# Two feed-forward networks behind a clustered attention: the order of instructions written out as a list

## The chip, the cores and the metric

One core of a Trainium2 chip. The metric is the device time of one execution in microseconds (us), as the median of several runs; lower is better. Engines: TensorE (PE), VectorE (DVE), ScalarE (ACT), GpSimd (POOL) and SyncE (SP), which issues the loads.

## The reference

```python
x = attention(q, k, v)              # 2 x 8 heads, 768 tokens, masked by clusters
h = x @ w_in                        # x: 1536 x 512, w_in: 512 x 2048
g = where(h >= 1, h, where(h <= -1, 0, (h + 1)**2 / 4))
x = g @ w_out                       # 1536 x 512
xn = x / sqrt(mean(x*x) + 1e-6) * rms_g
g = silu(xn @ w_gate) * (xn @ w_val)    # 512 x 1536 each
out = g @ w_out2                    # 1536 x 512
```

Everything is float32.

## The kernel before, in words

The attention takes up to about 250 us and isn't touched. Behind it stand two feed-forward networks (FFN), layers 1 and 2. Each factor is split into a high part that the multiplier takes (type fp32r) and a low rest, and a product is three matmuls: high by high, high by low, low by high. The tokens are three blocks of 512 (b = 0, 1, 2), the hidden columns slices of 128 (m).

*Units.* TensorE's work is a list of units. `h_unit` computes one slice for one block (12 matmuls of 512 columns). For blocks 0 and 1 `term_unit` computes a Strassen-like scheme: seven products of six matmuls each (called k = 1, 5, 2, 6, 3, 7, 4), added up in three PSUM banks A, B and E. Partial sums are copied out by ScalarE as u (after k = 1), e (5), v (6) and w (7, line 918), and added by DVE or POOL later (lines 924, 929). Product 3 adds to the bank E and so needs the copy e first; product 6 needs u, 7 needs v, 4 needs w. In layer 2, `half_unit` does the same for the halves of block 2 with 256 columns (names with h; copies in line 963). `y_unit` multiplies a group of slices with the second weight for 128 tokens (lines 1128 to 1130; y1 and y2; groups of 3, 4, 3, 3, 3 slices, and of 2), and the result is added to Y by DVE (line 1144; the first by a copy of ScalarE, line 1142). Between the layers come the norm (lines 1169 to 1174, 1181) and transposes of Y (xt, line 1066).

*Helpers.* Each unit leaves tasks for the other engines: gate or silu, the rounding to the high part by ScalarE (line 866) and the low rest by DVE (line 864), copies and additions. Weights come in as raw and mid by SyncE's loads (line 549), and are converted by two activations of ScalarE (lines 722, 723) and five steps of DVE (lines 724 to 728; into places named aa, bb or place); the last step of a conversion issues the load two places on (`load_next`). Sums of weights for the scheme are made by POOL (lines 739, 754, 755) and rounded (lines 716, 717).

*What sets the order.* `ORDER` permutes the units. The helpers are ordered by a planner: `KINDS` gives each operation an engine, a duration and a lag, each task has a due time, and before each unit `run` issues all operations that by its clock could have started, the one with the earliest due time first. A unit whose factor isn't planned yet pulls it in with `wait_for`, and `refill` begins the next weight conversion as soon as there is a place.

```python
    while unit():
        pass
    run(1e9)
```

PSUM has six banks of tag h (A, E, h, y, xt) and two of tag B; the buffers of other kinds are few (two of raw and mid each, four of u). An engine waits for a buffer's last reader in the order in which it was issued.

Of the kernel before, what the change touches and what calls it, by code (L numbers as in the profile page):

```python
# [32 lines left out]
SHARED, XP = 0.8, 1  # L33
KEEP, YD, GD, ROUND, XD, END4 = 1.5, 6.0, 6.0, 6.0, 2.0, 0.0
ORDER = (
# [21 lines left out]
NEAR, DUE, CONV = 0.1, 8.0, 4.0  # L57
LOAD, LAND = 4.2, 0.8
# [8 lines left out]
def clustered_attention_two_ffn(  # L67
# [509 lines left out]
    def conv(n_ops=1):  # L577

        for _ in range(n_ops):
# [12 lines left out]
            while cv["loaded"] < cv["limit"] and cv["loaded"] <= cv["at"]:  # L592
# [10 lines left out]
    def due_of(key):
        at = pace["pe"]
        for u in work:
            if key in u[3]:
                return at - CONV
            at += u[1]
        return at

    def task(ready, *ops, late=0.0, end=None, due=None):

        due = ready + DUE if due is None else due
        tasks.append(SimpleNamespace(ready=ready, ops=list(ops), late=late, end=end, due=due))

    def op(kind, f, sets=(), needs=(), stage=0):
        return kind, f, sets, needs, stage

    spans = {"dve": [], "pool": []}

    def start_of(x):
        kind, _, _, needs, _ = x.ops[0]
        e = KINDS[kind][0]
        at = max([clock[e], x.ready, *(known[k] for k in needs)])
        other = "pool" if kind in ("ttl", "t2l", "tiny") else "dve" if e == "pool" else None
        for a, b in spans[other][-3:] if other else ():
            if a <= at < b:
                at += SHARED * (b - at)
        return at

    def emit(x):
        kind, f, sets, needs, stage_ = x.ops[0]
        for k in needs:
            want(k)
        e, busy, lag = KINDS[kind]
        at = start_of(x)
        x.ops.pop(0)
        f()
        clock[e] = at + busy
        if e == "pool" or kind in ("ttl", "t2l", "tiny"):  # L640
            spans[e].append((at, at + busy))
        x.ready = at + lag
        if x.ops and x.ops[0][4] > stage_:
            x.due += ROUND
        for k in sets:
            known[k] = x.ready
        if not x.ops:
            tasks.remove(x)
            if x.end:
                x.end()  # L650

    def want(key):
        while key not in known:
            x = [x for x in tasks if any(key in o[2] for o in x.ops)]
            assert x, key
            emit(x[0])
        return known[key]

    def wait_for(*keys):
        for k in keys:  # L660
            pace["pe"] = max(pace["pe"], want(k) + 0.1)

    def run(until):
        while True:
            refill()
            heads = {}
            for n, x in enumerate(tasks):
                if any(k not in known for k in x.ops[0][3]):
                    continue
                at = start_of(x)  # L670
                if at < until:
                    heads.setdefault(KINDS[x.ops[0][0]][0], []).append((at, n, x))
            best = None
            for e, xs in heads.items():
                first = min(a for a, _, _ in xs) + NEAR
                a, n, x = min((y for y in xs if y[0] <= first), key=lambda y: (y[2].due, y[1]))
                if best is None or a < best[0]:
                    best = a, x
            if best is None:
                break  # L680
            emit(best[1])
# [12 lines left out]
    def load_next():
        while cv["loaded"] < len(stream) and stream[cv["loaded"]][2] < 0:
            cv["loaded"] += 1
        n = cv["loaded"]
        if n < len(stream):
            layer, i, m = stream[n]
            b = bound.setdefault("bits", [])  # L700
            bind("bits", 3, None)
            w_load()
            clock["dma"] = max(clock["dma"], pace["pe"] + 1.0) + LOAD
            landed[n] = clock["dma"] + LAND

    landed = {}

    def make():
# [13 lines left out]
        task(landed[n], op("copy", lambda: nc.scalar.activation(sq, hi.bitcast(F32), AF.Copy, scale=2.0 ** -112), (("y", n),)),  # L722
# [870 lines left out]
    for k in known:  # L1593
        known[k] = 0.0
# [70 lines left out]
```

## Time and profile before

| | us |
|---|---|
| median of 3 runs | 780.74 (780.57 to 780.75) |
| profiled execution | 779.35 |
| its span in the profile | 777.4 |
| PE busy in it | 763.2 (98%) |
| DVE busy | 630.2 (81%) |
| ACT busy | 468.0 (60%) |
| POOL busy | 330.3 (42%) |
| PE's granted clock, mean | 0.998 |

The span reaches from the first instruction to the last; 1.95 us of the profiled execution lie around it. PE is busy nearly all the time, so a seam is found by the starts of its matmuls: where they follow one another at the steady distance, PE loses nothing.

### The profile page before, as it was taken

Reading aid. Unit: us, or ns where it says so; the run is one execution under the profiler, and the core shown is the slowest. Engines: PE = TensorE matmul, PEld = TensorE weight load, DVE = VectorE, ACT = ScalarE, POOL = GpSimd, SP = SyncE. Lnnn points to the kernel's source line nnn. Section 1 sums busy time; section 2 is a strip of 40 time slices with the busy share of each in tenths; the row PEclk is TensorE's granted clock in tenths of the full one; section 3 lists DMA queues with packets and bytes.
Section 4 is the critical chain, followed back from the end, with each engine's and each line's share of the span. In section 5 each row is a group of like instructions: output and inputs, shape, how many; then the busy total and the mean of one; then the engine's idle time right before and its main releaser. Section 6 shows DMA issues by size and latency. Waiting matters only on the chain.

```text
span 777.4 us, 11522 instructions
## 1 busy us (share of the span) xinstructions
PE 763.2 (98%) x3897; PEld 593.0 (76%) x3897; DVE 630.2 (81%) x1164; ACT 468.0 (60%) x930; POOL 330.3 (42%) x344
## 2 busy tenths in 40 slices
PE   8999999999999989999999999899999999999998
PEld 4666676766558767888888888688888888888886
DVE  6776787776677979888889999999998798888545
ACT  6676767665565769548548358667754536365250
POOL 5878999998000050330400036455524333341220
PEclk9999999999999999999999999999999999999999
DMA  7757665572143155443452620336535344442004
GB/s 193 180 139 183 154 159 127 144 183 100 55 162 122 31 187 177 149 162 109 162 174 99 225 100 2 109 109 207 172 136 188 111 152 124 140 154 82 0 1 163
DMA packets 32682, 103.45 MB, mean 133 GB/s; under 512 B 5016, under 2 KB 5356, under 8 KB 32624
## 3 DMA queue, kind: packets, MB, share of 16 engines
q1 hardware_dynamic: 32612, 102.72, 43.5%
q8 instruction: 31, 0.51, 0.3%
q14 instruction: 27, 0.22, 0.1%
q10 hardware_dynamic: 12, 0.00, 0.0%
HBM read 81.02 MB, written 3.15 MB: 108 GB/s over the span
## 4 chain that ended last, share of the span: by engine, by line
PE 74%; DVE 16%; ACT 6%; issue 2%; DMA 1%; POOL 0%; DVEq 0%; ACTq 0%; POOLq 0%
PE B L848 9%; PE pv L432 8%; PE y L1130 7%; PE y L1128 7%; PE y L1129 7%; PE mp L362 5%; PE E L848 4%; PE sc L411 4%; PE sc L412 4%; PE h L789 3%; PE A L848 2%; DVE a L839 2%; PE sum L451 1%; DVE Y L1144 1%; ACT a L828 1%
## 5 line engine op out<-in xcount | busy, mean ns | idle before, releaser
L364 DVE TENSOR_REDUCE M<-mp 128x1 f32<-128x384 f32 x186 | 94.5, 552 | 44.5 <-PE mp L362 44.3
L424 POOL TENSOR_TENSOR acc<-acc,P 128x384 f32<-128x384 f32 x112 | 109.5, 1016 | 4.1 <-ACT P L414 3.5
L414 ACT ACTIVATE P<-sc 128x384 f32<-128x384 f32 x192 | 82.4, 490 | 41.7 <-PE sc L412 36.2
L739 POOL TENSOR_TENSOR bits<-aa 128x512 f32<-128x512 f32 x16 | 23.0, 1440 | 159.7 <-DVE aa L728 152.9
L1144 DVE TENSOR_TENSOR Y<-y,Y 128x512 f32<-128x512 f32 (+1 forms) x109 | 73.0, 678 | 8.9 <-PE y L1130 8.4
L432 PE MATMUL pv<-P,v 128*64 128x384 f32 x384 | 70.6, 492 | 0.0
L929 POOL TENSOR_TENSOR w<-w,e 128x512 f32<-128x512 f32 x17 | 24.2, 1422 | 108.3 <-ACT w L918 108.3
L411 PE MATMUL sc<-aa,bb 112*128 112x384 f32 x192 | 66.2, 345 | 0.0
L412 PE MATMUL sc<-aa,bb 97*128 97x384 f32 x192 | 65.0, 338 | 0.0
L789 PE MATMUL h<-xh,aa 128*128 128x512 f32 x200 | 64.3, 391 | 0.1
L739 POOL TENSOR_TENSOR bits<-place 128x512 f32<-128x512 f32 x13 | 18.3, 1407 | 85.5 <-DVE place L728 79.8
L362 PE MATMUL mp<-bb,aa 112*128 112x384 f32 x186 | 52.5, 360 | 0.2
L722 ACT ACTIVATE raw<-raw 128x512 f32<-128x512 f32 x62 | 41.5, 677 | 13.3 <-DMA raw<-w_out 6.9
L432 PEld LDWEIGHTS pv<-P,v 128*64 128x64 f32 x384 | 25.4, 136 | 31.5 <-issue 30.5
L789 PEld LDWEIGHTS h<-xh,aa 128*128 128x128 f32 x200 | 37.5, 188 | 9.9 <-DVE a L839 0.8
L362 PEld LDWEIGHTS mp<-bb,aa 112*128 112x128 f32 x186 | 32.2, 189 | 15.2 <-issue 5.5
L723 ACT ACTIVATE raw<-raw 128x512 f32<-128x512 f32 x62 | 41.8, 679 | 1.1
L789 PE MATMUL h<-xl,aa 128*128 128x512 f32 x100 | 39.0, 390 | 0.0
L411 PEld LDWEIGHTS sc<-aa,bb 112*128 112x128 f32 x192 | 36.3, 189 | 3.3 <-ACT P L414 1.4
L412 PEld LDWEIGHTS sc<-aa,bb 97*128 97x128 f32 x192 | 36.3, 189 | 0.0
L724 DVE TENSOR_SCALAR mid<-mid 128x512 uint32<-128x512 uint32 x62 | 33.5, 547 | 2.5 <-DMA mid<-w_out 1.8
L725 DVE TENSOR_SCALAR bits<-raw 128x512 uint32<-128x512 uint32 x62 | 34.3, 557 | 1.4 <-ACT raw L722 1.4
(678 smaller groups left out, 2239.2 us busy)
## 6 DMA issues: line engine op xcount, KB each, us to landing
raw<-w_out SPq DMA_DIRECT2D x28, 512.0 KB
mid<-w_out SPq DMA_DIRECT2D x28, 511.8 KB
raw<-w_in SPq DMA_DIRECT2D x16, 512.0 KB
mid<-w_in SPq DMA_DIRECT2D x16, 511.8 KB
raw<-w_gate SPq DMA_DIRECT2D x12, 512.0 KB
raw<-w_val SPq DMA_DIRECT2D x12, 512.0 KB
mid<-w_gate SPq DMA_DIRECT2D x12, 511.8 KB
mid<-w_val SPq DMA_DIRECT2D x12, 511.8 KB
```

The costliest lines, as they stand in the source:

```text
L362: nc.tensor.matmul(mp, A[0:112, h, 0, 128 * qt:128 * qt + 128], Bk[0:112, h, 0, HALF * n:HALF * n + HALF], start=True, stop=True)
L364: nc.vector.tensor_reduce(st["M2", p][:, j, n:n + 1], mp, axis=AX.X, op=ALU.max)
L411: nc.tensor.matmul(sc, Bk[0:112, h, 0, ks], A[0:112, h, 0, qs], start=True, stop=False)
L412: nc.tensor.matmul(sc, Bk[0:97, h, 1, ks], A[0:97, h, 1, qs], start=False, stop=True)
L414: nc.scalar.activation(P, sc, AF.Exp, scale=0.125)
L424: nc.gpsimd.tensor_tensor(acc, acc, P, op=ALU.add)
L432: nc.tensor.matmul(pv[64 * h:64 * h + 64, 0:HALF], st["v", p][:, h, kt], st["P", p, i, h], start=(kt == 0), stop=(kt == NT - 1))
L789: nc.tensor.matmul(h, w[:, wi, fs], x[:, kc, cs], start=(n == 0), stop=(n == 11))
L848: nc.tensor.matmul(h[:, 0:x[xi].shape[2]], w[:, wi, fs], x[xi][:, kc], start=start and n == 0, stop=(n == 5), skip_group_check=not start)
L1128: nc.tensor.matmul(y[:, c], g[:, 0, fs], w[:, 0, c], start=(m == m0), stop=False)
L1129: nc.tensor.matmul(y[:, c], g[:, 0, fs], w[:, 1, c], start=False, stop=False)
L1144: nc.vector.tensor_tensor(Y[:, c], y[:, c], Y[:, c], op=ALU.add)
```

## The change

The planner goes. A tuple `ISSUE` of some 2,000 numbers says what is issued next: `U` the next unit, `M` the next weight conversion (its tasks are made), and a number n the next operation of task n (tasks count from 0 in the order in which they are made). `ORDER`, the order of the units, is another one in places. The distances by which a needed value must be known are now asked for exactly: `have` replaces `wait_for`, and a layer 2 product needs only the part of x that it reads (`x_key`).

```diff
-SHARED, XP = 0.8, 1
-KEEP, YD, GD, ROUND, XD, END4 = 1.5, 6.0, 6.0, 6.0, 2.0, 0.0
+UNIT, MAKE = -1, -2
+U, M = UNIT, MAKE
+ISSUE = (
+    M, M, U, U, U, U, U, U, 25, 11, 25, 15, 10, 8, U, 25, 10, 11, 27, 11, 7, 26, 11, U, 8, 28, 13, 26, 19, 25,
...
+    620, U, 621, U, 622, U, 623, U, 624, U, 625)
 ORDER = (
...
-    253, 254, 255, 256, 258, 257, 259, 260, 261, 262, 263, 264, 270, 265, 266, 267, 268, 269, 272, 273, 271,
...
+    255, 256, 270, 258, 257, 259, 260, 261, 262, 263, 264, 265, 266, 267, 268, 269, 272, 273, 271, 274, 276,
...
-    def task(ready, *ops, late=0.0, end=None, due=None):
...
+    def task(*ops, end=None):
+
+        tasks[made[0]] = SimpleNamespace(ops=list(ops), end=end)
+        made[0] += 1
...
+    def emit(n):
+        x = tasks[n]
+        f, sets, needs, _ = x.ops.pop(0)
+        have(*needs)
         f()
...
+        known.update(sets)
         if not x.ops:
-            tasks.remove(x)
+            del tasks[n]
             if x.end:
                 x.end()
...
+    def have(*keys):
+        assert not pace["on"] or known.issuperset(keys), keys
...
+    def x_key(k, t):
+        return {1: ("tp0", t), 2: ("tp0", t), 3: ("xd", t)}.get(k) or ("xl", t, {5: 0, 6: 1, 7: 2, 4: 3}[k])
...
-            wait_for(*((("xl" if k in (5, 6, 7, 4) else "xd"), t) for t in range(4)))
+            have(*(x_key(k, t) for t in range(4)))
...
-    while unit():
-        pass
-    run(1e9)
-    assert not tasks
+    for n in ISSUE:
+        if n == UNIT:
+            work.pop(0)[0]()
+        elif n == MAKE:
+            make()
+        else:
+            emit(n)
+    assert not work and not tasks
```

Only the order of instructions differs. Line numbers above 700 are some 3 to 25 lower after the change (848 is 827, 1066 is 1044, 1128 is 1103; 722 is 725). Three places show it.

ScalarE at the slice pair m = 3 of layer 1 (the names end in a running number; e1_3 is the copy e, v1_3 the copy v, a1_3_2 the gated slice 3 of block 2, bb0 the place of its high part). Before:

```order
L723 ACTIVATE raw11_3331<-raw11_3331 128x512
L828 ACTIVATE a1_3_2_3441<-h1_3_2_3414,half_b_93 128x512
L835 ACTIVATE a1_3_2_3441<-a1_3_2_3441 128x512
L866 CAST bb0_106<-a1_3_2_3441 128x512
L918 COPY e1_3_3458<-E1_3_3451 128x512
L828 ACTIVATE a1_3_0_3473<-A1_3_3433,half_b_93 128x512
L722 ACTIVATE raw12_3408<-raw12_3408 128x512
L918 COPY v1_3_3470<-B1_3_3397 128x512
```

ScalarE at the same place after the change:

```order
L726 ACTIVATE raw15_3388<-raw15_3388 128x512
L898 COPY e1_3_3461<-E1_3_3454 128x512
L1014 CAST place1_3129<-p3_0_3291 128x512
L807 ACTIVATE a1_3_2_3474<-h1_3_2_3425,half_b_93 128x512
L898 COPY v1_3_3473<-B1_3_3409 128x512
L814 ACTIVATE a1_3_2_3474<-a1_3_2_3474 128x512
L807 ACTIVATE a1_3_0_3487<-A1_3_3442,half_b_93 128x512
L814 ACTIVATE a1_3_0_3487<-a1_3_0_3487 128x512
L898 COPY w1_3_3503<-B1_3_3409 128x512
L1014 CAST place1_3129<-p3_1_3313 128x512
L719 CAST aa0_105<-s1_5_1_3440 128x512
L807 ACTIVATE a1_3_1_3512<-E1_3_3454,half_b_93 128x512
```

The copy e1_3 stood behind the gate and the rounding of a1_3_2 (L866, CAST). Now the gate stands behind the copy, and the rounding follows two rows below the last one shown. Between come a weight's two activations and casts of x parts (L1014).

TensorE at the norm (layer 2; B_0 and B_1 belong to slices 0 and 1, the two xt are the transposes of Y's tiles 8 and 10, of 128 tokens each). Before:

```order
L848 MATMUL B_0_5305<-aa_109,place_3131 128x512
L1066 MATMUL xt_5393<-ident_f,Y 128x128 x4
L1066 MATMUL xt_5398<-ident_f,Y 128x128 x4
L848 MATMUL B_1_5414<-xh,place_3133 128x512
L848 MATMUL B_1_5414<-xl,place_3133 128x512
L848 MATMUL B_1_5414<-xh,place_3133 128x512 x2
L848 MATMUL B_1_5414<-xl,place_3133 128x512
```

TensorE there after the change:

```order
L827 MATMUL B_1_5393<-xh,place_3133 128x512
L827 MATMUL B_1_5393<-xl,place_3133 128x512
L827 MATMUL B_1_5393<-xh,place_3133 128x512 x2
L827 MATMUL B_1_5393<-xl,place_3133 128x512
L827 MATMUL B_1_5393<-xh,place_3133 128x512
L827 MATMUL A_1_5406<-xh,place_3133 128x512
L827 MATMUL A_1_5406<-xl,place_3133 128x512
L827 MATMUL A_1_5406<-xh,place_3133 128x512 x2
L827 MATMUL A_1_5406<-xl,place_3133 128x512
L827 MATMUL A_1_5406<-xh,place_3133 128x512
L1044 MATMUL xt_5415<-ident_f,Y 128x128 x4
L1044 MATMUL xt_5420<-ident_f,Y 128x128 x4
```

The transposes stood directly behind the last unit of slice 0 and now stand behind the first two units of slice 1 (B_1 and A_1), each of six matmuls.

TensorE at the half products of slices 0 and 1. Before:

```order
L848 MATMUL B_0h<-bb_106,place_3131 128x256 x6
L848 MATMUL B_0h<-bb_108,place_3129 128x256 x6
L848 MATMUL B_1h<-xh,place_3133 128x256
L848 MATMUL B_1h<-xl,place_3133 128x256
L848 MATMUL B_1h<-xh,place_3133 128x256 x2
L848 MATMUL B_1h<-xl,place_3133 128x256
L848 MATMUL B_1h<-xh,place_3133 128x256
L848 MATMUL A_1h<-xh,place_3133 128x256
```

TensorE there after the change:

```order
L827 MATMUL B_0h<-bb_106,place_3131 128x256 x6
L827 MATMUL B_1h<-xh,place_3133 128x256
L827 MATMUL B_1h<-xl,place_3133 128x256
L827 MATMUL B_1h<-xh,place_3133 128x256 x2
L827 MATMUL B_1h<-xl,place_3133 128x256
L827 MATMUL B_1h<-xh,place_3133 128x256
L827 MATMUL B_0h<-bb_108,place_3129 128x256 x6
L827 MATMUL A_1h<-xh,place_3133 128x256
```

The third and fourth product in the bank B_0h followed each other directly; now B_1h's first product stands between them. In the same way y2_0_4, the first unit of y2, now stands between B_1h's last two products. Other moves on TensorE: E2_0 stands ahead of A2_0; the first unit of each later pair (B2_4, B2_6, B2_8, B2_10) stands ahead of the y2 group that it used to follow for seven units; the second unit of B2_11 stands ahead of E2_11h. Up to the norm TensorE's order is the same, and so is that of SyncE's loads throughout.

## Rows read from the trace of the kernel before

**Rows 1.** The page, busy time of each engine (share of the span), instructions:
```profile
PE 763.2 (98%) x3897; PEld 593.0 (76%) x3897; DVE 630.2 (81%) x1164; ACT 468.0 (60%) x930; POOL 330.3 (42%) x344
```

**Rows 2.** PE's waits, 238 to 778 us: total, times, longest:
```profile
PE xt L1066 <- DVE Y L1181: 2.9, 1, 2.9
PE E L848 <- ACT e L918: 2.9, 1, 2.9
PE B_0h L848 <- ACT w_0h L963: 1.0, 1, 1.0
PE B_1h L848 <- ACT w_1h L963: 0.5, 1, 0.5
...
```

**Rows 3.** PE in stretches: width, busy (instructions), granted clock, DMA share, GB/s:
```profile
290.00:300.00 10.00, 10.00 (x45) 1.00 0.31 106
255.88:265.31 9.43, 9.02 (x38) 1.00 0.01 2
282.31:289.80 7.49, 4.64 (x19) 1.00 0.69 216
307.49:311.29 3.80, 3.28 (x14) 1.00 0.65 225
436.45:438.97 2.52, 2.33 (x10) 1.00 0.28 86
493.59:496.72 3.13, 3.02 (x13) 1.00 0.82 285
496.72:508.39 11.67, 8.74 (x41) 0.85 0.01 4
501.00:504.00 3.00, 2.83 (x11) 0.50 0.02 5
507.60:508.39 0.79, 0.79 (x9) 1.00 0.00 0
519.10:521.85 2.75, 1.70 (x14) 1.00 0.60 191
521.85:525.51 3.66, 3.66 (x32) 1.00 0.13 19
525.51:527.72 2.21, 1.69 (x14) 1.00 0.69 248
574.26:574.99 0.73, 0.73 (x3) 1.00 0.24 90
```

**Rows 4.** ScalarE's timeline at E1_3 and at B_1h: start, duration, line, operation:
```profile
281.95 0.63 ACT L835 ACTIVATE a<-a 128x512 f32<-128x512 f32 x1
285.52 0.62 ACT L866 CAST bb<-a 128x512 fp32r<-128x512 f32 x1 [2.94 <-DVE a L839]
286.05 0.58 ACT L918 COPY e<-E 128x512 f32<-128x512 f32 x1
...
526.48 0.37 ACT L963 COPY w_1h<-B_1h 128x256 f32<-128x256 f32 x1 [0.31 <-PE B_1h L848]
```

**Rows 5.** PE's timeline, 500 to 503 us:
```profile
501.17 1.94 PE L1066 MATMUL xt<-ident_f,Y 128*128 128x128 f32 x8 [2.93 <-DVE Y L1181]
```

**Rows 6.** VectorE's timeline at the end of the norm:
```profile
499.02 1.22 DVE L1174 SCALAR_TENSOR_TENSOR rr<-rt,rr 128x4 f32<-128x4 f32 x1
500.27 1.42 DVE L1181 SCALAR_TENSOR_TENSOR Y<-Y,rr,gain 128x512 f32<-128x512 f32 x2
```

**Rows 7.** Two stretches: width, then busy PE, PEld, DVE, ACT, POOL, clock, DMA, GB/s:
```profile
280.00:310.00 30.00, 26.83 (x116) 21.24 (x115) 28.51 (x49) 26.45 (x48) 7.76 (x7) 1.00 0.54 175
490.00:530.00 40.00, 35.40 (x193) 30.16 (x192) 37.88 (x74) 25.80 (x56) 20.08 (x21) 0.96 0.35 119
```

**Rows 8.** Line 725 alone, 238 to 778 us: duration minimum/median/maximum:
```profile
L725 DVE TENSOR_SCALAR bits<-raw x62: 411/418/1555, 267.5 to 719.4; 128x512 uint32<-128x512 uint32 x62
```

**Rows 9.** The chain of waits, 420 to 440 us:
```profile
430.57 4.40 DMA mid<-w_out
```

**Rows 10.** VectorE's timeline, last step of the conversion of B2_4's weight:
```profile
551.17 0.69 DVE L728 SCALAR_TENSOR_TENSOR aa<-mid,bits 128x512 fp32r<-128x512 uint32 x1
```

More of the change, by code (lines that the diff above doesn't have):

```diff
@@ L603, in due_of @@
[L603 to L609, printed above, removed]
-    def task(ready, *ops, late=0.0, end=None, due=None):
[L613 to L637, printed above, removed]
-        f()
[L639 to L646, printed above, removed]
+    tasks, known, later = {}, set(), set()
@@ L659, in wait_for @@
[L659 to L681, printed above, removed]
@@ L696, in load_next @@
             cv["loaded"] += 1
[L697 to L701, printed above, removed]
+        if cv["loaded"] < len(stream):
             w_load()
-            clock["dma"] = max(clock["dma"], pace["pe"] + 1.0) + LOAD
-            landed[n] = clock["dma"] + LAND
-    landed = {}
     def make():
@@ L738, in w_sums @@
         g = nc.gpsimd.tensor_tensor
-        first = op("p512", lambda: g(f, w[:, 0].bitcast(F32), w[:, 1].bitcast(F32), op=ALU.add), (("f", layer, i, m),), (("w0", key), ("w1", key)))
+        first = op(lambda: g(f, w[:, 0].bitcast(F32), w[:, 1].bitcast(F32), op=ALU.add), (("f", layer, i, m),), (("w0", key), ("w1", key)))
         k1, k2 = ("s", layer, 0, -m - 1), ("s", layer, 1, -m - 1)
-        bound["bits"][[n for n in range(len(bound["bits"]))][-1]] = None
         if i == 0:
             fp["f"] = f
-            task(0.0, first, due=due_of(key))
+            task(first)
             return
@@ L792, in hbank @@
     def hbank(name, key):
-        if pace["on"]:
-            bind("h", HB, key)
         return fp["h"](name)
     def abuf(name, key):
-        if pace["on"]:
-            bind("a", AB, key)
         return fp["a"](name)
     def ubuf(name, key):
-        bind("u", 4, key)
         return pf.tile([128, 512], F32, tag="u", bufs=4, name=name)
-    def now(us):
-        return pace["pe"] + us + 0.15
     def x_ready(layer, b):
         if layer == 2 and b == NB - 1:
-            wait_for(*(("x", t) for t in range(8, 12)))
+            have(*(("x", t) for t in range(8, 12)))
         if layer == 1 and b == 1 and "back" in fp:
-            wait_for(("back", 0), ("back", 1))
+            have(("back", 0), ("back", 1))
     def h_unit(layer, m, b):
@@ L864, in low @@
             e.tensor_tensor(g[:, 1], fp["g", m, b], g[:, 0].bitcast(F32), op=ALU.subtract)
-        return (op("copy", lambda: nc.scalar.copy(g[:, 0], fp["g", m, b]), stage=1),
-                op("p512" if slow else "ttl", low, (("G", layer, m, b),), stage=1))
+        return (op(lambda: nc.scalar.copy(g[:, 0], fp["g", m, b]), stage=1),
+                op(low, (("G", layer, m, b),), stage=1))
     def silu(m, b, x):
@@ L896, in term_unit @@
         if layer == 2:
-            wait_for(*((("xl" if k in (5, 6, 7, 4) else "xd"), t) for t in range(4)))
+            have(*(x_key(k, t) for t in range(4)))
         elif k in (5, 6, 7, 4):
-            wait_for(*(("xt", {5: 1, 6: 2, 7: 3, 4: 4}[k], j) for j in range(2)))
+            have(*(("xt", {5: 1, 6: 2, 7: 3, 4: 4}[k], j) for j in range(2)))
         bank = "bank", c, layer, m
@@ L907, in term_unit @@
         if k in (6, 7, 4, 3):
-            wait_for(("keep", {6: "u", 7: "v", 4: "w", 3: "e"}[k], layer, m))
+            have(("keep", {6: "u", 7: "v", 4: "w", 3: "e"}[k], layer, m))
         x = {1: (0, 0), 5: (0, 1), 2: (2, 0), 3: (2, 1)}.get(k)
@@ L934, in term_unit @@
         elif row == 0:
-            last = (op("copy", lambda: silu(m, b, src), (bank, ("a", m, b))),)
+            last = (op(lambda: silu(m, b, src), (bank, ("a", m, b))),)
         else:
-            last = (op("tt", lambda: times(m, b, C["w", m] if k == 7 else src), (end_,), (("a", m, b),)), *rounded(2, m, b))
-        task(now(1.36), *first, *last, due=now(1.36) + (END4 if k == 4 and layer == 2 else GD))
+            last = (op(lambda: times(m, b, C["w", m] if k == 7 else src), (end_,), (("a", m, b),)), *rounded(2, m, b))
+        task(*first, *last)
     def half_unit(k, m):
@@ L946, in half_unit @@
             fp["g", m, 2] = abuf(f"a2_{m}_2", ("G", 2, m, 2))
-        wait_for(*((("xl" if k in (5, 6, 7, 4) else "xd"), t) for t in (8, 9)))
+        have(*(x_key(k, t) for t in (8, 9)))
         bank, h = ("half", c, m), ("half", m)
@@ L951, in half_unit @@
         if k in (6, 7, 4, 3):
-            wait_for(("keep", {6: "u", 7: "v", 4: "w", 3: "e"}[k], h))
+            have(("keep", {6: "u", 7: "v", 4: "w", 3: "e"}[k], h))
         x = {1: (0, 0), 5: (0, 1), 2: (2, 0), 3: (2, 1)}.get(k)
@@ L1119, in y_unit @@
         ws = [need((layer, layer, m)) for m in ms]
-        wait_for(*(("G", layer, m, b) for m in ms))
+        have(*(("G", layer, m, b) for m in ms))
         n_cols = 2 if layer == 2 and n + 1 == len(groups) and t == last_t(layer, n) else 1
@@ L1146, in add @@
                     nc.sync.dma_start(out[128 * t:128 * t + 128, c], Y[:, c])
-        ops = [op("tt" if n else "copy", add, (("y", layer, n, t),), (("y", layer, n - 1, t),) if n else ())]
+        ops = [op(add, (("y", layer, n, t),), (("y", layer, n - 1, t),) if n else ())]
         if n + 1 == len(groups) and layer == 1:
-            ops.append(op("sq", lambda: norm_sq(t), (("ssq", t),)))
-        task(now(0.68 * len(ms)), *ops, due=now(0.68 * len(ms)) + YD)
+            ops.append(op(lambda: norm_sq(t), (("ssq", t),)))
+        task(*ops)
     def drain():
-        for x in list(tasks):
-            k = x.ops[0][4] if x.ops else 0
-            while x.ops and x.ops[0][4] == k:
-                emit(x)
+        for n in list(tasks):
+            k = tasks[n].ops[0][3]
+            while n in tasks and tasks[n].ops[0][3] == k:
+                emit(n)
     def norm_sq(t):
@@ L1339, in room @@
         return True
-    pace = {"on": False, "pe": 0.0}
+    pace = {"on": False}
     def unit():
-        if not work:
-            return False
-        if pace["on"]:
-            run(pace["pe"])
-        else:
-            drain()
-        f, us, _, _, _ = work.pop(0)
-        f()
-        if pace["on"]:
-            pace["pe"] += us
-        return True
+        drain()
+        work.pop(0)[0]()
     PREP0 = [12 * p - 30 for p in range(NP)]
```

277 lines of the change are left out of this document (159 added, 118 removed), and 38 rows, old and new, of the table ORDER.

## The prediction

> **What bounds the kernel now.** I read the busy times first: TensorE (PE) is busy 763.2 of 777.4 us, VectorE (DVE) 81% [rows 1]. So the kernel can only get shorter where PE stands still or runs slow. The list of PE's waits behind the attention shows where: two of 2.9 us, one of 1.0, one of 0.5 [rows 2], 7.3 us together; three smaller ones follow. But a wait costs more than its idle time: the matmuls behind it are slow as well. So I measured every seam from start to start, against the undisturbed cadence. That cadence is 45 matmuls in 10.00 us, one of which began before, so 0.227 us for 512 columns; 30 matmuls of 256 columns in 3.66, so 0.122; eight transposes in 0.79 [rows 3]. A unit of six is then 1.36, a half unit 0.73. The count in a row includes one or two matmuls that began before its window; I take the number that the code issues between the two starts.
>
> Lost per seam [rows 3]:
> - S1, four units of y1_0, 36 matmuls: 9.43 − 8.16 = 1.27 (the bank waits for ScalarE's Y copy).
> - S2, from 282.31, 18 matmuls: 7.49 − 4.08 = 3.41 (E1_3 waits for the copy e).
> - S3, 307.49, 12: 3.80 − 2.72 = 1.08 (y1_1_8 waits for a rounding).
> - S4, 436.45, 9: 2.52 − 2.04 = 0.48 (y1_4_0 waits for a converted weight).
> - S5, 493.59, 12: 3.13 − 2.72 = 0.41 (E2_0).
> - S6, the norm seam from 496.72, 24 and 16 transposes: 11.67 − 5.44 − 1.58 = 4.65.
> - S7, 519.10, 12 half: 2.75 − 1.46 = 1.29; S8, 525.51: 2.21 − 1.46 = 0.75 (B_0h and B_1h wait for the copies w).
> - S9, the third matmul of a y2 group on a late rounding: 0.73 − 0.45 = 0.28, and five groups look like this: 1.4.
>
> Together 14.7 us; 6.2 in the first FFN (S1 to S4), 8.5 in the second. In S6, only 2.93 of the 4.65 is idle [rows 5]; afterwards the granted clock was 0.50 from 501 to 504, the 1.2 GHz level, where the other stretches show 1.00 (and the whole seam 0.85) [rows 3]. The wait of about the same length in S2 lowered nothing. So the clock's part of S6 goes only if the wait goes.
>
> **The change, part by part.** No instruction is added or removed, and SyncE's loads stand in the same order; all gain is from order. Up to about 250 us nothing moves: 0. The last y2 group and the tail keep their order: 0.
>
> *S1.* ScalarE's Y copies now stand ahead of the casts of x parts. Before, the casts stood between them; without these the copies are done before PE wants the bank. Gain 1.27, covered by the unit of nine (2.04) that runs meanwhile.
>
> *S2.* ScalarE stood 2.94 us before the cast bb←a, because DVE came late to a L839, and the copy e was behind it at 286.05 [rows 4]. Now e stands right behind a weight's two activations and the cast far behind. e could begin when E1_3's first unit ends, about 282.5, and be done at 283.1 with its 0.58 [rows 4]; the six matmuls from 282.31 end at 283.67. Slack 0.6, so 3.41 gained. In exchange the cast of a1_3_2 is late; who waits for it is y1_1_8 at 307.49, 21 us on. If weight 15 has not landed, its two activations hold e up instead: the price is that of a late load, 4.40 [rows 9], and stands in the upper bound.
>
> *S3, S4.* The rounding and the weight conversion come earlier by several instructions each; 1.08 and 0.48 gained, covered by the units in between.
>
> *S5, S6.* E2_0 goes ahead of A2_0, so the copy e has one unit more, 1.36 against 0.41 lost: gained. Two units (B2_1, A2_1; 2.72) now stand between the last B2_0 and the transposes xt8 and xt10. DVE's chain to the scaled Y had a step of 1.22 on a 128x4 tile, and the first two scalings end at 501.69 [rows 6]. The two units end 2.72 behind the start of the old wait, 501.17 − 2.93 = 498.24, at 500.96. If DVE's chain is no earlier than before, xt8 waits 0.2 for 501.17 [rows 5] and xt10 0.3 more for 501.69. It should be earlier, since E2_0's addition, in its midst before, now stands behind the first two scalings. I take 4.65 as gone, and 0.5 as the bound of what stays. The scaling for xt11 now comes three instructions later than the one before it, which makes it tight (below).
>
> *S7, S8.* Between B_0h's third and fourth product now stands B_1h's first (0.73), between those of B_1h the unit y2_0_4 (1.36). How much cover is needed, S8 tells: there ScalarE sat idle until B_1h was ready and copied in 0.37 [rows 4], and it lost 0.75. So 1.36 covers it fully, and 0.73 nearly (0.02 left), if ScalarE is free; one cast of 0.62 ahead of it is the bound. y2_0_4 begins a half unit and a wait sooner by this, and needs its rounded factors 1.5 us sooner. Gain 2.0.
>
> *S9.* The next pair's first unit B2_4 (6, 8, 10) stands ahead of the group, so the roundings have 1.36 more against 0.28: gain 1.4 (the fifth group gets its unit from the second B2_11, moved ahead of E2_11h). It asks for B2_4's weights seven units, 9.5 us, sooner; they were finished at 551.86 [rows 10], some 21 us before the seam at 573. Cost 0.
>
> *What is newly tight.* Laying the new order on the old durations by hand, four places keep under 0.3 us: the copy v of E1_3's slice, the transposes xt11, E2_0h's low part of x, and the copy w of B_0h. DVE is what makes them late: its step bits←raw has a median of 0.418 but a maximum of 1.555 us [rows 8], a stretch of 1.14. Bounds: 0, and one stretch at each, 4 × 1.14 = 4.5. The median says that stretches are rare, the crowded place says that they are not rare here; I take two, less their slack: 2.0.
>
> Sum: −14.7 + 2.0 = −12.7, so 779.35 − 12.7 = 766.65 for an execution like the profiled one. That one lies 1.39 below the median of the runs; in their terms it is 780.74 − 12.7 = **768.0 us**.
>
> The Trainium skill, "SBUF — State Buffer", section "SBUF: two separate sides", says that VectorE and GpSimd take one shared pair of ports as an exclusive lock for a whole instruction, and that the loser fully blocks. The stretch in [rows 8] agrees with it. By that rule every one of the four tight places would be hit, since GpSimd's additions still run beside the conversions: 780.74 − 14.7 + 4.5 = 770.5, an estimate.
>
> **Rivals.**
> 1. *VectorE becomes the bound.* It is busy 37.88 of 40 us in 490 to 530, and 28.51 of 30 in 280 to 310 [rows 7]. If PE's losses there go (7.1 of S5 to S8, 4.5 of S2 and S3), 32.9 and 25.5 us remain for the same work: 5.0 and 3.0 would come back as new waits. −14.7 + 8.0 = −6.7: **774.0**. For it: the two busiest stretches are those of the largest gains. Against: what is late there can wait (conversions and roundings for later units), and PE's waits in these stretches were for single instructions, not for a queue.
> 2. *Slower: weights come late.* The end of each conversion issues the load two places on. The list moves conversions and asks for the four units B2_4 to B2_10 9.5 us sooner. A load that is waited for cost 4.40 [rows 9]. If each of the four waits so, 17.6 − 12.7 = +4.9: **785.6**. It decides from the fourth on; three give +0.5, no change. Against: the finish at 551.86 [rows 10].
> 3. *Only the second FFN gains.* In the first PE's order is the same, and all rests on helpers that get elsewhere in the way. −8.5: **772.2**, within a tenth or two.
> 4. *Waits only move*: the list reproduces the planner's waits elsewhere, **780.7**. Against: the moved rows stand exactly at the waits.
>
> **How the numbers follow.** A measurement of this kernel tells about 0.2%, 1.6 us, from no change. Forecast (766 to 770.5) 0.58; rival 1 0.15; rival 3 0.13; rival 4 0.06; rival 2 0.08. Faster 0.86, same 0.06, slower 0.08. The range begins at 780.74 − 14.7 = 766.0, less 0.5 for the small waits that I did not count, and reaches over the bound of the tight places (770.5) and rival 3 to rival 1: 765.5 to 774.
>
> **What would show it.** Right: no wait of PE above 0.5 us behind 250 us; transposes xt8 directly behind A2_1, the granted clock at 1.00 there; each group of S9 at cadence; y2_0_4 at 526.24 − 12.6 (S1 to S7) = 513.6, or up to 2.0 later. Rival 1: waits on DVE between the norm and the first y2 unit, DVE busy to 99% there. Rival 2: PE, ScalarE or DVE waiting for raw or mid just before B2_4 to B2_10. Rival 3: waits left at 255 to 310. Wrong at all: a sum of PE's waits no smaller than 7.3.

## The result and the profile after

| | before | after |
|---|---|---|
| median, us | 780.65 (4 runs, 780.04 to 780.75) | 771.5 (4 runs, 770.55 to 772.37) |
| profiled execution, us | 779.35 | 771.4 |
| its span, us | 777.4 | 769.6 |
| DVE busy, us | 630.2 | 636.2 |

The ratio is 0.9884, 95% interval [0.9867, 0.9901]: faster by 1.2%, 9.15 us in the medians and 7.8 in the two profiled spans. Forecast were 768.0 and −12.7, range 765.5 to 774.0. One execution of k9_room, at a granted clock of 0.75 throughout, is left out below.

The page and the list of PE's waits after the change, which answer to [rows 1] and [rows 2]:

```profile
PE 759.9 (99%) x3897; PEld 594.0 (77%) x3897; DVE 636.2 (83%) x1164; ACT 473.2 (61%) x930; POOL 342.0 (44%) x344
```

```profile
PE E L827 <- DVE aa L720: 2.3, 1, 2.3
PE E_1h L827 <- ACT e_1h L942: 1.3, 1, 1.3
PE B L827 <- ACT v L898: 0.3, 1, 0.3
```

All four waits shown of before are gone, and of the three new ones two are long. PE in stretches after the change (width, busy, granted clock, DMA share, GB/s), which answers to [rows 3]:

```profile
256.10:264.26 8.16, 8.16 (x37) 1.00 0.52 194
279.90:288.05 8.15, 5.90 (x19) 0.79 0.12 43
307.12:309.84 2.72, 2.72 (x13) 1.00 0.83 292
434.96:437.00 2.04, 2.04 (x10) 1.00 0.75 261
494.30:501.43 7.13, 7.13 (x42) 1.00 0.02 7
512.18:514.40 2.22, 2.22 (x20) 1.00 0.21 35
515.84:518.03 2.19, 0.88 (x8) 1.00 0.85 247
518.85:521.67 2.82, 2.82 (x20) 1.00 0.65 232
568.05:569.74 1.69, 1.64 (x8) 1.00 0.27 99
```

In the order of the rows: S1 takes 8.16, its 36 matmuls at cadence. The 18 matmuls of S2 (from E1_3's first unit on) take 8.15 where 4.08 would do. S3 (2.72) and S4 (2.04) are at cadence, the norm seam nearly (7.13 against 7.02); B_0h's and B_1h's turns (2.22 and 2.82) are at cadence too. New is the stretch from 515.84, six half matmuls in 2.19 instead of 0.73. The last row is the one y2 group that still loses, 1.69 against 1.36. The clock of 0.79 is a mean: behind PE's wait it was 0.50, the 1.2 GHz level, from 283 to 286, and 1.00 before and after.

To settle each term I laid the starts of the same units side by side. After the change they are these rows of PE's timeline (y1_0_3, E1_3, y1_1_9, B2_0, B_0h, y2_0_5, y2_5_4):

```profile
256.10 0.39 PE L1103 MATMUL y<-bb 128*128 128x512 f32 x1
...
279.90 0.39 PE L827 MATMUL E<-xh,aa 128*128 128x512 f32 x1
...
309.84 0.39 PE L1103 MATMUL y<-bb,bb 128*128 128x512 f32 x1
...
487.50 0.39 PE L827 MATMUL B<-xh,place 128*128 128x512 f32 x1
...
506.96 0.28 PE L827 MATMUL B_0h<-xh,place 128*128 128x256 f32 x1
...
521.67 0.40 PE L1103 MATMUL y<-bb,aa 128*128 128x512 f32 x1
...
749.88 0.40 PE L1103 MATMUL y<-aa,bb 128*128 128x512 f32 x1
```

Before, they stand at 255.88, 280.94, 311.29, 489.51, 514.13, 529.11 and 757.36. Between two starts the same matmuls run, so the difference of the lengths is what was won:

| from, to | terms | forecast | before | after | won |
|---|---|---|---|---|---|
| y1_0_3, E1_3 | S1 | 1.27 | 25.06 | 23.80 | 1.26 |
| E1_3, y1_1_9 | S2, S3 | 4.49 | 30.35 | 29.94 | **0.41** |
| y1_1_9, B2_0 | S4 | 0.48 | 178.22 | 177.66 | 0.56 |
| B2_0, B_0h | S5, S6 | 5.06 | 24.62 | 19.46 | 5.16 |
| B_0h, y2_0_5 | S7, S8 | 2.04 | 14.98 | 14.71 | **0.27** |
| y2_0_5, y2_5_4 | S9, four of five | 1.1 | 228.25 | 228.21 | **0.04** |
| y2_5_4, end | S9, the fifth | 0.28 | 20.04 | 19.72 | 0.32 |

The sum is 8.02, less 0.22 by which y1_0_3 starts later: 7.8, the difference of the spans. Three places did not give what was forecast (in bold). The experiments are about the first two, and undo the moves on TensorE at the norm and at the y2 groups. An order that reads "unchanged" does not repeat to the tenth: the attention, whose order never differs, ends between 255.2 and 257.5 in the profiles below, which alone moves a time by 2 us. So I judge by these lengths and by waits, and by times only where they differ by more.

### The profile page after: what moved, and what is told of

Same layout as the page of the kernel before. It is cut to its first block, busy times and chain, and to the rows that moved or that the text cites. A ratio compares the mean times of both kernels' runs of the same rounds, so it can differ in the third digit from the quotient of the medians.

```text
span 769.6 us, 11540 instructions
## 1 busy us (share of the span) xinstructions
PE 759.9 (99%) x3897; PEld 594.0 (77%) x3897; DVE 636.2 (83%) x1164; ACT 473.2 (61%) x930; POOL 342.0 (44%) x344
## 4 chain that ended last, share of the span: by engine, by line
PE 83%; DVE 11%; DMA 3%; issue 2%; ACT 1%; DVEq 0%; ACTq 0%
PE h L776 10%; PE B L827 9%; PE y L1105 8%; PE pv L515 8%; PE y L1103 8%; PE y L1104 8%; PE mp L445 5%; PE E L827 5%; PE sc L494 4%; PE sc L495 4%; PE A L827 2%; PE sum L534 1%; DMA mid<-w_gate 1%; PE simt L280 1%; DVE bits L728 1%
## 5 line engine op out<-in xcount | busy, mean ns | idle before, releaser
L741 POOL TENSOR_TENSOR bits<-aa 128x512 f32<-128x512 f32 x17 | 25.1, 1480 | 150.1 <-DVE aa L731 135.4
L741 POOL TENSOR_TENSOR bits<-place 128x512 f32<-128x512 f32 x10 | 15.2, 1516 | 71.9 <-DVE place L731 71.9
L727 DVE TENSOR_SCALAR mid<-mid 128x512 uint32<-128x512 uint32 x62 | 31.5, 510 | 3.9 <-DMA mid<-w_gate 3.0
L503 POOL TENSOR_TENSOR acc<-P,P 128x384 f32<-128x384 f32 x28 | 27.7, 1011 | 14.0 <-ACT P L497 14.0
```

## The experiments

All are the changed kernel with its list edited (in k4, k8 and k10 the order of the units too); the control is the changed kernel itself, run again. Of the lines named ahead of the prediction, 716 to 728 are 3 higher after the change: 719 and 720 round a sum of weights, 725 and 726 are a weight's activations, 727 to 731 the steps of its conversion; 847 and 845 round a gated slice, 898 and 942 are the copies, 1007 to 1015 make parts of x.

> The changed kernel as it is, as the control for its variants on the same chip: 771.5 by every theory.

Measured: 770.83 us (5 runs, 769.2 to 772.83), ratio 0.9876 [0.9859, 0.9894]. Its profile has the same two long waits (2.2 and 1.3); E1_3 to y1_1_9 takes 30.03, B_0h to y2_0_5 14.73.

### The stretch from E1_3 to y1_1_9

PE waits there for a low part of a weight sum (aa, L720). VectorE's timeline after the change, from 278 us, and GpSimd's beside it:

```profile
278.04 0.68 DVE L720 TENSOR_TENSOR aa<-s,aa 128x512 fp32r<-128x512 f32 x1
278.64 1.81 DVE L1015 TENSOR_TENSOR xl<-p,xh 128x512 fp32r<-128x512 f32 x1
280.37 1.21 DVE L1015 TENSOR_TENSOR bb<-p,bb 128x512 fp32r<-128x512 f32 x1
281.51 1.21 DVE L720 TENSOR_TENSOR aa<-s,aa 128x512 fp32r<-128x512 f32 x1
282.64 1.22 DVE L1015 TENSOR_TENSOR bb<-p,bb 128x512 fp32r<-128x512 f32 x1
```

```profile
281.12 1.05 POOL L754 TENSOR_TENSOR s<-s,bits 128x256 f32<-128x256 f32 x1
282.13 1.18 POOL L755 TENSOR_TENSOR s<-bits,bits 128x256 f32<-128x256 f32 x1
283.26 1.19 POOL L756 TENSOR_TENSOR s<-bits,s 128x256 f32<-128x256 f32 x1
```

The low part that PE waits for is the one that starts at 281.51. Ahead of it stand two parts of x, and they take 1.81 and 1.21, where the row above takes 0.68. Beside them GpSimd adds up weights, 256 columns in 1.05 to 1.19 (its median for such additions behind 250 us is 0.93, its shortest 0.73). The starts interlock: 280.37, 281.12, 281.51, 282.13, 282.64, 283.26. Each engine begins its next instruction 1.0 to 1.1 us behind its last one, in turns with the other. VectorE itself never stands idle for over 0.15 us between 270 and 312 us.

**k1_low_first**: what is wanted first goes first.

```diff
 VectorE
-L720 aa2 <- s1_3_1 (low), L1015 xl <- p0_1, L1015 bb1 <- p2_1, L720 aa2 <- s1_3_0 (low), L1015 bb1 <- p2_0
+L720 aa2 <- s1_3_0 (low), L1015 xl <- p0_1, L1015 bb1 <- p2_0, L1015 bb1 <- p2_1, L720 aa2 <- s1_3_1 (low)
```

> The changed kernel (771.5 us) with three of VectorE's roundings in another order: the low part of E1_3's weight sum (wanted first) goes ahead of an x part and of the other weight sum's low part, which is wanted three units later. Nothing else moves. Theory A (the 2.25 us wait of E1_3 in the changed kernel is the list's order: VectorE does what is wanted later first): the low part is done near 279 instead of 282.7, the wait at E1_3's first unit is gone, a wait of about 1.2 us is left one unit later where x's parts are late, and without the long wait the clock stays at 1.00: 771.5 - 3.9 + 1.2 = 768.8. Rival B (VectorE is the bound in this stretch, any order of it ends equally late): the wait only moves to the next unit, 771.5.

Measured: 769.77 us, ratio 0.9868 [0.9845, 0.9890]. The wait at E1_3 is gone, and others came at the next units: 0.18 for a part of x, and two long ones:

```profile
284.47 0.50 PE L827 MATMUL E<-xh,aa 128*128 128x512 f32 x1 [1.12 <-ACT e L898]
...
287.82 0.50 PE L827 MATMUL B<-bb,aa 128*128 128x512 f32 x1 [1.69 <-ACT v L898]
```

The stretch takes 29.96 against 29.94: nothing won in it. Theory A falls, rival B holds. The time is nearer to A's 768.8, but not for A's reason: the profile won 1.5 us between y2_0_5 and y2_5_4 (226.71 against 228.21), where the list is the same. The copy e waits for its turn behind a cast (L719) that waited 1.47 for GpSimd's sum until 282.05, and behind a weight's two activations. The clock, 0.79 over the stretch after the change, stayed at 1.00 here and nothing was gained by that either: in the changed kernel the slow matmuls only covered what would have been waited for the copy v. k3 and k10, with the changed kernel's list there and the clock at 1.00, wait 1.25 and 1.28 for it.

**k2_conv_later**: GpSimd's additions moved away.

```diff
 VectorE
-conversion 11, steps L729, L730, L731   (ahead of five parts of x and weight sums)
+the same, behind them
 ScalarE
-L719 cast of s1_5_0, L725 and L726 of raw15   (ahead of the copies e1_3 and v1_3)
+the same, behind them
```

> The changed kernel with the order of those roundings untouched, but the last three steps of weight conversion 11 (which nothing wants for long), GpSimd's additions that hang on it, and the next weight's two activations on ScalarE moved behind them. Theory C (VectorE's subtractions take 1.2 to 1.8 us instead of 0.69 there because GpSimd's additions run beside them): with GpSimd idle they take 0.69, the low part of E1_3's weight is done near 278, no wait of E1_3: 771.5 - 3.9 = 767.6. Rival B (the bound is VectorE's work, which only moves by 3 us): the wait comes back at the next units, 770 to 771.5.

Measured: 769.69 us, ratio 0.9869 [0.9849, 0.9890]. VectorE's timeline in it:

```profile
277.84 0.69 DVE L1015 TENSOR_TENSOR xl<-p,xh 128x512 fp32r<-128x512 f32 x1
278.44 0.69 DVE L1015 TENSOR_TENSOR bb<-p,bb 128x512 fp32r<-128x512 f32 x1
279.04 0.69 DVE L720 TENSOR_TENSOR aa<-s,aa 128x512 fp32r<-128x512 f32 x1
279.64 0.69 DVE L1015 TENSOR_TENSOR bb<-p,bb 128x512 fp32r<-128x512 f32 x1
```

Theory C's mechanism is shown: with GpSimd idle (its next addition starts at 282.32) the same subtractions take 0.69, and E1_3 doesn't wait. Little of its gain comes: 29.14 in the stretch, 0.8 won instead of 3.9, since waits of 1.3 (copy v) and 1.4 (a part of x) come later.

**k5_first_ffn**: k2's edits, and the copy v and x's fourth part ahead of casts, gates and the end of conversion 12.

```diff
 ScalarE, behind copy e1_3 and with k2's edits made
-cast p3_0, gate a1_3_2, copy v1_3, ... gate a1_3_0, copy w1_3, cast p3_1
+copy v1_3, cast p3_0, gate a1_3_2, ... cast p3_1, gate a1_3_0, copy w1_3
 VectorE
-L730, L731, L1007 of p3_1, L727, two gates, L1015 place <- p3_1 (low)
+L1007 of p3_1, L730, L731, L727, L1015 place <- p3_1 (low), two gates
```

> k2_conv_later with its two remaining waits taken up: ScalarE's copy v of slice pair 3 ahead of a cast that waits for VectorE and of a gate, and the subtraction, cast and low part of x's fourth part ahead of a weight conversion's last steps and of two gates. Theory F (the waits of 282 to 292 us are a chain through ScalarE's and VectorE's order, and there is slack once it is put in the order in which TensorE asks): the v wait (1.4) and the wait for x's part (1.5) are gone, nothing from 270 to 295 waits: 769.7 - 3.1 = 766.6. Rival B (VectorE and ScalarE are full): they come back one or two units later, 769.7.

Measured: 770.42 us, ratio 0.9877 [0.9860, 0.9894]; a wait of 2.5 us for the copy w came in their place, since ScalarE had a gate and a cast that waits for VectorE ahead of it. The stretch takes 30.24. (k7 below, with the same list there and the same wait, takes 29.47; its clock stayed at 1.00 behind the wait, where k5 shows 0.58 from 290 to 294.)

**k9_room** and **k11_room_again**: all of conversion 12 behind x's fourth part, the copy w ahead of the gates (with the edits of k2 and, below, of k6).

```diff
 ScalarE, behind copy e1_3
-cast p3_0, gate a1_3_2, copy v1_3, ... copy w1_3, cast p3_1
+copy v1_3, cast p3_0, cast p3_1, copy w1_3, gate a1_3_2, ...
 VectorE
-L727 to L731 of conversion 12   (among and ahead of L1015 place <- p3_0, p3_1)
+the same, behind them
-L731, L845 aa <- a2_1_1, ... L945 A_1h <- A_1h, u_1h
+L945 A_1h <- A_1h, u_1h, L845 aa <- a2_1_1, L731, ...
```

> k7_both with room made for VectorE from 280 to 290 us, where it is busy 19.6 of 20 us: all five steps of weight conversion 12, which nothing asks for before 300, go behind x's fourth part; on ScalarE the casts of that part and the copy w go ahead of two gates, a rounding and a weight's activations; in the second FFN VectorE's addition to A_1h (whose late end holds the buffer of the copy w_1h) goes ahead of a low part. Theory F (VectorE was the bound there only because conversions that can wait were packed into it): the wait of 2.5 us at w and that of 0.6 at w_1h go: 769.6 - 2.7 - 0.8 = 766.1. Rival B (whatever is put off comes due before VectorE has caught up, up to 310): 769.6.

> The kernel of k9_room once more, whose profile came from an execution with the whole clock at 0.75 and so tells nothing of its waits. Theory F (room for VectorE removes the waits from 280 to 292 us): none of PE's waits between 270 and 300 is over 0.3 us. Rival B (what is put off comes due later): a wait as long stands behind 292, at the units that use weight 12, the sums for pair 5 or the gates that were put off, and the time is no better than 769.6.

Measured: 772.82 us (5 runs), ratio 0.9907 [0.9885, 0.9929], and again 772.56 us, 0.9903 [0.9876, 0.9930]. The list of PE's waits of k11, and all engines in two stretches of it (width, then busy PE, PEld, DVE, ACT, POOL, clock, DMA, GB/s):

```profile
PE y L1103 <- ACT aa L847: 1.6, 1, 1.6
PE E L827 <- ACT e L898: 1.3, 2, 0.8
PE B L827 <- ACT u L898: 1.0, 1, 1.0
PE y L1105 <- DVE bb L845: 0.5, 1, 0.5
...
```

```profile
270.00:295.00 25.00, 25.00 (x112) 20.70 (x111) 24.62 (x37) 18.64 (x34) 8.94 (x7) 1.00 0.36 112
295.00:312.00 17.00, 13.47 (x55) 9.57 (x54) 16.25 (x30) 16.60 (x29) 0.69 (x1) 1.00 0.57 199
```

Up to 295 us PE is busy 25.00 of 25: the room is made. From 295 to 312 it then loses 3.5 us, in waits of 0.8 to 1.6 for copies and roundings, and the stretch takes 30.82, the longest of all. So rival B: what is put off is paid behind. VectorE is busy 24.62 of 25 up to there, then 16.25 of 17; but then ScalarE, with 16.60 of 17, is the fuller one: it has no idle time over 0.15 us from 294.1 to 312 (the gates that were put off, and a table load of 1.28 us at 308.84, directly ahead of the rounding that PE waits 1.6 for), while VectorE waits 0.51 us for it. So the bound there passes from VectorE to ScalarE. That VectorE is the bound up to there is argued from its busy time and from waits that only move; no run takes work off it. The same stretch (width, busy PE, PEld, DVE, ACT, POOL and the rest) before, after, and in k11:

```profile
270.00:311.00 41.00, 37.62 (x164) 29.96 (x162) 34.24 (x59) 31.43 (x56) 13.93 (x14) 1.00 0.56 186
```

```profile
270.00:311.00 41.00, 38.75 (x165) 31.50 (x164) 40.23 (x67) 35.41 (x63) 10.09 (x8) 0.96 0.48 154
```

```profile
270.00:311.00 41.00, 37.52 (x162) 29.81 (x161) 39.87 (x65) 34.48 (x61) 8.94 (x7) 1.00 0.43 143
```

The list put 6 us more of VectorE's work into these 41 us than the planner had: 40.23 us are busy, against 34.24, in 67 instructions against 59.

### The half products

ScalarE after the change around the new wait, and the unit of PE that waits:

```profile
515.93 0.62 ACT L847 CAST bb<-a 128x512 fp32r<-128x512 f32 x1 [1.69 <-DVE a L856]
516.53 0.62 ACT L847 CAST aa<-a 128x512 fp32r<-128x512 f32 x1
517.05 0.67 ACT L725 ACTIVATE raw<-raw 128x512 f32<-128x512 f32 x1
517.63 0.35 ACT L942 COPY e_1h<-E_1h 128x256 f32<-128x256 f32 x1
```

```profile
518.03 0.39 PE L827 MATMUL E_1h<-xh,aa 128*128 128x256 f32 x1 [1.31 <-ACT e_1h L942]
```

The copy e_1h, which can start when PE ends E_1h near 516.0, stands behind two roundings (which waited for VectorE until 515.93) and a weight's activation. PE waits 1.31. VectorE is busy 38.88 of the 40 us from 490 to 530.

**k3_e_first** and **k6_half_copies**: the copies go first.

```diff
 ScalarE
-cast bb1 <- a2_1_0, cast aa0 <- a2_1_1, raw53, copy e_1h, copy v_1h, raw53
+copy e_1h, copy v_1h, cast bb1 <- a2_1_0, cast aa0 <- a2_1_1, raw53, raw53       (k3)
+copy e_1h, copy v_1h, cast aa0 <- a2_1_1, cast bb1 <- a2_1_0, copy w_1h, raw53, raw53  (k6)
 VectorE (k6)
-L731, L845 aa <- a2_1_1
+L845 aa <- a2_1_1, L731
```

> The changed kernel with ScalarE's copies e_1h and v_1h put ahead of two roundings and one weight's activation that stood before them (and one low part of VectorE behind its rounding). Theory A (the 1.31 us wait of E_1h's second product is ScalarE's order alone): wait gone, 771.5 - 1.5 = 770.0, and nothing behind it later. Rival B: ScalarE and VectorE are full there, the roundings that now come later hold up y2_0_4 instead: 771.5.

> The changed kernel with ScalarE's copies e_1h, v_1h and w_1h ahead of the roundings, the silu and the weight's activations around them, and VectorE's low part that y2_0_4 needs ahead of the last step of conversion 52. Theory F: the wait of 1.31 us at E_1h goes, and the two that took its place in k3_e_first (0.42 and 1.04) don't come: 771.5 - 1.6 = 769.9. Rival B: they move again, 771.5.

Measured: 771.35 us, 0.9890 [0.9870, 0.9909], and 772.25, 0.9902 [0.9885, 0.9918]. By the times neither is told from the control. By the lengths k3 lost (15.31 against 14.71), since waits of 0.42 and 1.04 came at y2_0_4 and B_1h:

```profile
521.77 0.49 PE L1105 MATMUL y<-aa,aa 128*128 128x512 f32 x1 [0.42 <-DVE aa L845]
...
523.30 0.98 PE L827 MATMUL B_1h<-bb,aa 128*128 128x256 f32 x6 [1.04 <-ACT w_1h L942]
```

k6 won 0.5 (14.19), with one wait of 0.6 left for w_1h. Before that copy ScalarE stood idle for 1.59 us, until VectorE had made its addition to A_1h. In k11, where this addition also goes earlier, the length is 13.32: all waits from B_0h to y2_0_5 gone, 1.4 us won. But they are not won for good. Behind y2_0_5 k11 waits again, for a low part of VectorE and for a copy e:

```profile
528.71 0.50 PE L1105 MATMUL y<-aa,bb 128*128 128x512 f32 x1 [0.54 <-DVE bb L845]
...
547.66 0.50 PE L827 MATMUL E<-xh,aa 128*128 128x512 f32 x1 [0.53 <-ACT e L898]
```

By the starts these two cost 0.82 and 0.80, all of the 1.4. k6 loses 0.33 and k7 0.57 at the second of these matmuls; none of the other nine profiles with a list loses there. So here, too, rival B holds: the waits move, only farther.

**k7_both**: k5 and k6 together.

> k5_first_ffn and k6_half_copies together. Theory F: 766.6 - 1.6 = 765.0, about what the prediction's sum gives with nothing left over (766.0). Rival B: 769.7.

Measured: 769.57 us, the fastest, ratio 0.9869 [0.9852, 0.9886]; its interval overlaps the control's, so that it beats the changed kernel isn't shown. Stretches 29.47 and 14.17.

**k8_undo_turns**: B_1h's first product behind B_0h's last, y2_0_4 behind B_1h's last.

```diff
 PE   (k is the product's number)
-B_0h (7), B_1h (1), B_0h (4), ... B_1h (7), y2_0_4, B_1h (4)
+B_0h (7), B_0h (4), B_1h (1), ... B_1h (7), B_1h (4), y2_0_4
```

> The changed kernel with the half products back in their old turns on TensorE: B_1h's first product behind B_0h's last, y2_0_4 behind B_1h's last. By the terms S7 and S8 of the prediction the whole 2.0 us come back: 771.0 + 2.0 = 773.0. Theory G (each product now waits only for its copy, 0.75 each, since ScalarE is free at B_0h, and the first of these waits shortens the 1.3 us that E_1h waits for its copy): 771.0 + 1.5 - 0.75 = 771.8. A rival that the turns bring nothing: 771.0.

Measured: 771.36 us, 0.9890 [0.9873, 0.9907]. B_0h to y2_0_5 takes 15.46 instead of 14.73, 0.7 more, as theory G has it: waits of 0.52 (w_0h) and 0.46 (w_1h) return, and E_1h waits 0.62 instead of 1.33:

```profile
514.48 0.98 PE L827 MATMUL B_0h<-bb,place 128*128 128x256 f32 x6 [0.52 <-ACT w_0h L942]
...
518.95 0.39 PE L827 MATMUL E_1h<-xh,aa 128*128 128x256 f32 x1 [0.62 <-ACT e_1h L942]
```

So the two waits that the turns were to remove (S7, S8) are removed by them, and most of their worth went into the wait at E_1h.

### The norm seam and the groups

**k4_undo_norm**: xt8 and xt10 ahead of B2_1 and A2_1 again.

```diff
 PE
-B2_1, A2_1, xt8, xt10
+xt8, xt10, B2_1, A2_1
```

> The changed kernel with one unit moved back on TensorE: the transposes xt8 and xt10 stand directly behind slice 0's last unit again, ahead of B2_1 and A2_1. Theory D (most of the 4.65 us of the norm seam was won by VectorE's chain, which now ends near 497, and only the rest by the two units in between): the transposes wait 1.1 us for Y8 and 0.3 more for Y10, 771.5 + 1.4 = 772.9, or about 1.6 more where the clock falls behind the wait: 774.5. Rival E (the two units cover it all, as the prediction put it): the whole term comes back, 771.5 + 4.65 = 776.2.

Measured: 773.83 us, 0.9922 [0.9903, 0.9942], an interval above the control's; B2_0 to B_0h takes 23.86 where the others have 19.5 to 19.9: 4.0 more. PE's two waits and VectorE's two scalings:

```profile
496.37 0.63 PE L1044 MATMUL xt<-ident_f,Y 128*128 128x128 f32 x4 [1.04 <-DVE Y L1156]
498.03 0.92 PE L1044 MATMUL xt<-ident_f,Y 128*128 128x128 f32 x4 [1.03 <-DVE Y L1156]
```

```profile
495.47 2.50 DVE L1156 SCALAR_TENSOR_TENSOR Y<-Y,rr,gain 128x512 f32<-128x512 f32 x2
```

The two scalings together took 2.50, where they took 1.42 [rows 6] (an addition of GpSimd, 1.26 us from 496.16, runs beside them), so xt10 waited 1.0 and not 0.3; and the clock was 0.50 behind the waits. By the length, 4.0, this is nearer to rival E (4.65) than to theory D with the clock (3.0); by the time, 3.0 above the control, it is theory D's number. By the waits D is right in part: xt8 waits 1.04, as D has it, where it waited 2.93 before, so VectorE's chain alone came 1.9 us nearer. So both were needed, the earlier chain and the two units; without the units most of the term S6 comes back.

**k10_undo_groups**: B2_4, B2_6, B2_8 and B2_10 back behind seven y2 units.

```diff
 PE
-B2_4's first product, y2_1_4, y2_1_5, y2_1_6, y2_1_7, y2_1_0, y2_1_1, y2_1_2, y2_1_3
+y2_1_4, y2_1_5, y2_1_6, y2_1_7, y2_1_0, y2_1_1, y2_1_2, B2_4's first product, y2_1_3
 ScalarE
-copy u2_4   (behind the roundings of a2_3_1 and a2_3_0)
+the same, five or six instructions later   (both likewise for 6, 8 and 10)
```

> The changed kernel with the first unit of the four later pairs (B2_4, B2_6, B2_8, B2_10) back behind seven units of the y2 group on TensorE. By the term S9 four of its five seams come back, 4 x 0.28 = 1.1: 772.1. The rival is that ScalarE and VectorE now round earlier in the list and the unit in between is not needed: 771.0.

Measured: 774.62 us (6 runs, 773.18 to 775.77), 0.9933 [0.9916, 0.9951], 3.8 above the control, whose interval lies below this one. By the starts of the matmuls, measured as S9 was, the four seams lose 1.70, 1.01, 0.56 and 0.51, each more than the 0.28 of before, and 3.8 together; the first of them:

```profile
568.29 0.50 PE L1103 MATMUL y<-aa,bb 128*128 128x512 f32 x1 [0.73 <-ACT bb L847]
...
569.44 0.50 PE L1105 MATMUL y<-aa,bb 128*128 128x512 f32 x1 [0.42 <-DVE bb L845]
```

0.73 and 0.42 of waiting here, on a rounding and on its low part, where a seam like it lost 0.28 in all before [rows 3]. Without the unit in between, the list's roundings come too late. The move on PE and the list of the helpers only work together; what in the list makes the rounding later than under the planner wasn't pursued.

## Why the prediction came out as it did

The direction, the range and the reading of the seams were right: the nine places hold the loss, and S1, S4, S5, S6 and the fifth of S9 gave what was forecast within 0.1 (7.3 for 7.1 together; S5 and S6 won 5.2 here and 4.8 in the control, where xt11 waits 0.16). −9.15 came instead of −12.7, and the step that failed is "What is newly tight", in its size and in its places: it took 2.0 for four named places, and the lengths show 14.7 − 8.0 = 6.7. Of the four, none waits in the changed kernel's profile; the transposes xt11 wait 0.16 in the control, and the copy v is waited for where the clock stayed at 1.00 (k3, k10). The long waits came where the step has none: at the low part for E1_3 (2.25) and at the copy e_1h (1.31). Of the signs, the transposes stood directly behind A2_1 at a clock of 1.00; "no wait above 0.5" did not hold, and y2_0_4 began at 519.57 instead of 513.6 to 515.6.

- **S2, "Slack 0.6, so 3.41 gained".** Only the copy e was followed there. The low parts that E1_3 needs were on the same engine as the conversions pulled forward, and VectorE took 1.2 us where 0.69 is its time with GpSimd idle. The copy e had no slack either: in k1, with the low part in time, PE waited 1.12 for it. S3 won its 1.08, but S2 now loses 4.07 where it lost 3.41: 0.41 of 4.49 together.
- **Rival 1** was right in kind for 280 to 310: VectorE is full, and none of four other orders there (k1, k2, k5, k11) won more than 0.8 us. It gave 3.0 back, 4.1 came. For 490 to 530 it gave too much: 5.0 were to come back, 1.8 did (S7, S8). Its reason is there, though: the roundings ahead of e_1h waited for VectorE, and the orders that remove these waits wait again within 30 us.
- **S7, S8.** The copies of the two turns were covered, as worked out from S8. But the forecast looked at B_0h and B_1h's last product, and the wait came at E_1h, two units on.
- **S9.** The fifth group won its 0.28. In the other four the seams are closed but one (0.33), and losses of 0.57 (at 561) and 0.37 (at B_6h) stand elsewhere in the same 228 us; the length is the same as before. The order alone doesn't set this: with the same list there, k1, k2, k3, k5 and k8 took 226.7 to 226.9, so that 1.3 to 1.5 were won for the 1.1 forecast; the control took 228.2, k4 228.8 and k6 230.1. Why the same order waits in one execution and not in another stays open; k10 (230.8) shows that undoing the move costs more than it was to bring.
- **Rival 2** did not come: no wait for raw or mid. **Rival 3** came near in its number (772.2), by luck: the first FFN won 2.2 of 6.2, where it had nothing, and the second 5.8 of 8.5, where it had all. **Rival 4** is wrong for the whole by 8.0 us, but its mechanism, waits that only move, is what the experiments show in the first FFN and at the half products.
- The Trainium skill, "SBUF — State Buffer", section "SBUF: two separate sides", has an instruction of VectorE with two inputs in SBUF and one of GpSimd that reads SBUF share one port pair: whichever starts first holds it for the whole instruction, and the other fully blocks. The traces agree: the starts interlock, and with GpSimd idle the subtraction takes 0.69 (k2). Behind 250 us of the changed kernel's profile, 45 of the 146 two-input operations of VectorE (TENSOR_TENSOR, 128x512) with GpSimd at work beside them took over 0.9 us, up to 1.81; of the 227 others none took over 0.70. The estimate by that rule in the prediction, 770.5, was nearer than the forecast, but partly by luck: it charged the same four places.

## What to carry to other kernels

Closing seams of the busiest engine one by one is worth their sum only as long as the helper engines have slack in that stretch: look at the busy share over 20 to 40 us around a seam, and allow for 1.2 instead of 0.7 us for a two-input operation of VectorE (128x512) while GpSimd adds beside it, as in the rows above. Where VectorE is at 98%, moving one instruction forward moved the wait to the next units, or on to ScalarE. A gain read over a short length has to be read over the next 30 us as well (k11). A hand-written order ties engines together, so that undoing a single move can cost more than it brought (k10).

## What was not expected

- The same wait lowers the clock in one execution and not in another: behind 2.2 us of waiting at E1_3 the changed kernel, its control, k4, k6 and k8 ran at 0.50 for a while, k3 and k10 with the same wait at 1.00, and the kernel before stayed at 1.00 behind 2.85. The length of the stretch was the same with and without (29.94 after the change, 29.99 in k3, 29.93 in k10): at 1.00 PE waits for the copy v instead, which stands behind a cast that waited 1.65 for VectorE (k3).
- Equal orders spread by more than most terms: 769.2 to 772.83 in five runs of the control, and 777.84 to 781.15 in eleven runs of the kernel before that were taken beside it. Part of it is the attention's end (255.2 to 257.5), part single waits such as that for w_6h, 1.4 us in k4 and k6 and 0.1 at most in others with the same list there.
